# Turning the exponents of two batches, and the first block's normalised rows, by TensorE instead of by DMA

## The chip, the cores and the metric

The kernel runs on one core of one Trainium2 chip. The metric is the time of one execution on the device in microseconds (us), as the median over several runs. A profiled execution, taken by the hardware profiler, stands beside it; all rows shown here come from that execution. The engines are named as in the profile: PE is TensorE's matrix multiplication, PEld its load of the stationary operand, DVE is VectorE, ACT is ScalarE, POOL is GpSimd, and SP is the engine whose queue issues most DMAs.

## The reference

Four batches of 576 tokens pass through four steps. First comes attention with 8 heads of 64 columns, masked by blocks of 64 tokens, in 32 bits:

```python
scores = scale * np.matmul(q, k.transpose(0, 1, 3, 2))
scores = np.where(mask, scores, -1000000000.0)
scores = scores - np.max(scores, axis=-1, keepdims=True)
attn = np.exp(scores)
attn = attn / (np.sum(attn, axis=-1, keepdims=True) + 1e-09)
return np.matmul(attn, v)
```

Then comes a normalisation over the 512 columns, with a feed-forward layer 512 to 2048 to 512 behind it and a residual sum; then a two-dimensional Fourier transform of which the real part is added; then a second normalisation and feed-forward layer. The change touches the attention of the first 256 tokens of batches 0 and 1, and the normalisation in front of the first feed-forward layer for batch 0's first 256 tokens.

## The kernel before

The tokens are cut into blocks: E b holds tokens 0 to 255 of batch b (b is 0 to 3), F b and L the others. Attention of the E blocks runs first, a pair of heads p at a time (four pairs for a batch). A later stream does the attention of the other tokens. The first feed-forward layer takes its blocks in the order E0, E1, E2, E3, F0, and so on.

Matrix products keep nearly 32 bits by splitting each operand into a high and a low half of 16 bits and adding three products (high by high, high by low, low by high). So an operand of a product is first split by an ACT pass (the high half) and a DVE pass (the rest), and what has to be turned is turned as 16-bit halves by a transposing DMA on SP's queue.

For one pair of heads of an E block the steps are these. `e_raw` loads queries and keys in 32 bits by three DMAs and clears half of the key tiles on POOL. `e_s` multiplies them on PE, in 32 bits, into the PSUM tile `st` (two buffers), and `mask` adds the block mask. `e_exp` takes the row maxima (DVE) and the exponents (ACT) into `e`, 128 rows by 768 columns. `e_norm_p` splits `e` into the 16-bit tile `P` by `p_split` (L885 on ACT, L886 on DVE) and turns it by `p_turn`, a transposing DMA of 128 by 1536 elements (L892). `e_pv` multiplies the turned tile `PT` with the values on PE (L861, 18 products of at most 65 columns; column 65 is of ones and gives the row sums), and `e_x` divides and writes the block `X`. `e_load` brings a batch's values in one DMA (L836) into the tile `rv`, of which there is one buffer; `e_v` scales and splits them (L870, L873, L874, a sum over all partitions on POOL, and five small DVE steps).

`ln` makes a block's row means and scales, `ln_hi` the normalised rows `xn` and their high half `xs` (L568), `ln_lo` the low half (L574) and two transposing DMAs into `xnT` (L575). `gemm1` then multiplies `xnT` with the layer's first weights (L607), eight groups of 24 products, two groups for each quarter of the weights.

Beside this runs the decoding of the first layer's weights. `w_load` brings a piece of 1 MB (L198), `w_decode` makes 32-bit numbers of it (ACT L213, DVE L214, ACT L235), and `w_hi` and `w_lo` scale and split each quarter (ACT L327, DVE L335). `gemm1` of a quarter waits for that quarter.

Which work is laid beside which is set by `merge`: each stream has a start time and a rate in planned units, and the item with the earliest planned time is emitted next. E0 starts at 0, the weights at 20, E1 at 25, E2 and E3 at 50. Every engine then carries out its own instructions in the order that the build laid down, and waits at the head of its queue. `prio(f, n)` lets what f emits go n places earlier in that order. The E blocks' tiles come from a pool with a fixed number of buffers for each tag:

```python
a_open(dict(stage=ST, rv=RVE, raw=RAWE, vh=2, vl=2, e=E1B[0], P=E1B[1], PT=E1B[2], xnT0=1, xn0=X0B, xs0=X0B))
```

Here `rv` has one buffer, `raw` two, `e` three, `P` and `PT` two each.

Of the kernel before, what the change touches and what calls it, by code (L numbers as in the profile page):

```python
# [8 lines left out]
F32 = mybir.dt.float32  # L9
F16 = mybir.dt.float16  # L10
# [3 lines left out]
AF = mybir.ActivationFunctionType  # L14
ALU = mybir.AluOpType
# [3 lines left out]
DM = H * D  # L19
FF = 4 * DM  # L20
NPAIR = H // 2
KT = DM // 128
# [5 lines left out]
ST = 2  # L28
RVE = 1
RAWE = 2  # L30
# [11 lines left out]
E1B = (3, 2, 2)  # L42
NB = 1
P_D = 0
EL = 1
RKB = 2
PSC = 2.0 ** 14
WN = (2, 1)
# [5 lines left out]
X0B = 2  # L54
G1E = 1
LNA = 2
ESP = 20
# [38 lines left out]
def fused_kernel(ctx: ExitStack, tc: tile.TileContext, io: dict):  # L96
    nc = tc.nc
# [4 lines left out]
    fpool = ctx.enter_context(tc.tile_pool(name="fpool", bufs=1))  # L102
# [413 lines left out]
    xnT = {}  # L516
# [36 lines left out]
    def ln_hi(ffn, c, t):  # L553
        mv, y = lnst[ffn, c]
        own = (ffn, c) == (1, ("E", 0))
        if own:
            xn = a_tile([128, DM], F32, "xn0", "xn0")
        else:
            xn = fpool.tile([128, DM], F32, tag="xn", bufs=1, name="xn")
        nc.vector.tensor_scalar(  # L560
            out=xn, in0=X[c][:, t, :], scalar1=mv[:, t, 0:1], scalar2=y[:, t:t + 1],
            op0=ALU.subtract, op1=ALU.mult,
        )
        if own:
            xs = a_tile([128, 2, DM], F16, "xs0", "xs0")
        else:
            xs = fpool.tile([128, 2, DM], F16, tag="xs", bufs=1, name="xs")
        nc.scalar.activation(out=xs[:, 0, :], in_=xn, func=AF.Copy)  # L568
        lnst[ffn, c, t] = (xn, xs)

    def ln_lo(ffn, c, t):
        xn, xs = lnst.pop((ffn, c, t))
        eng = nc.gpsimd if (ffn, t) in LNP else nc.vector
        eng.tensor_tensor(out=xs[:, 1, :], in0=xn, in1=xs[:, 0, :], op=ALU.subtract)  # L574
        nc.sync.dma_start_transpose(  # L575
            out=xnT[ffn, c].rearrange("p a k t -> p (a k) t")[:, :, t * 128:(t + 1) * 128],
            in_=xs.rearrange("p a f -> p (a f)"),
        )
# [206 lines left out]
    A = {}  # L785
# [10 lines left out]
    def a_open(bufs):  # L796
        ap_["ctx"] = ExitStack()
        ap_["p"] = ap_["ctx"].enter_context(tc.tile_pool(name="apool", bufs=1))
        ap_["b"] = bufs

    def a_tile(shape, dt, tag, name):
        return ap_["p"].tile(shape, dt, tag=tag, bufs=ap_["b"][tag], name=name)
# [29 lines left out]


    def e_load(b):
        r = a_tile([128, NPAIR, 256], F32, "rv", f"rv{b}")
        nc.sync.dma_start(  # L836
            out=r.rearrange("k p (c d) -> k p c d", c=2),
            in_=io["vt"][b].rearrange("p k c d -> k p c d")[:, :, 0:2, :],
        )
        A["rv", b] = r  # L840
# [24 lines left out]
    def e_v(b):  # L865
        r = A.pop(("rv", b)).rearrange("k p (n d) -> k (p n) d", d=64)
        vh, vl = v_tiles(4 * NPAIR, f"{b}")
        vhf, vlf = vh[:, :, 0:64], vl[:, :, 0:64]
        n2 = sm.tile([128, 1], F32, tag="en", name="en")
        nc.scalar.activation(out=vhf, in_=r, func=AF.Square, accum_out=n2)  # L870
        tot = all_sum(n2, 1, "et")
        s, _ = pow2(tot, 1, "e")
        nc.scalar.activation(out=vhf, in_=r, func=AF.Copy, scale=s)  # L873
        nc.vector.scalar_tensor_tensor(  # L874
            out=vlf, in0=r, scalar=s, in1=vhf, op0=ALU.mult, op1=ALU.subtract
        )
        A["ev", b] = (vh, vl, s)
# [17 lines left out]
    def weights_of(sums, sv, shape, tag):  # L895

        w = sm.tile([128, 2] + shape, F32, tag="rr" + tag, bufs=3, name="rr")
        t, r = w[:, 0], w[:, 1]
        nc.vector.tensor_scalar(
            out=t, in0=sums, scalar1=1e-9 * PSC, scalar2=sv, op0=ALU.add, op1=ALU.mult  # L900
        )
        nc.vector.reciprocal(out=r, in_=t)
        return r
# [17 lines left out]
    def e_exp(b, p):  # L921
        st = A.pop(("st", b, p))
        e = a_tile([128, 2, 384], F32, "e", "e")
        q = sm.tile([128, 2, 2, 2], F32, tag="eq", bufs=3, name="eq")
        mx, nb = q[:, 0], q[:, 1]
        for t, (o, w) in enumerate(EO):
            nc.vector.tensor_reduce(out=mx[:, t], in_=st[:, :, o:o + w], axis=AX.X, op=ALU.max)
        nc.vector.tensor_scalar(out=nb, in0=mx, scalar1=-0.125, scalar2=None, op0=ALU.mult)
        for t, (o, w) in enumerate(EO):
            for h in range(2):  # L930
                nc.scalar.activation(
                    out=e[:, h, o:o + w], in_=st[:, h, o:o + w], func=AF.Exp, scale=0.125,
                    bias=nb[:, t, h:h + 1],
                )
        A["e", b, p] = e

    def e_norm_p(b, p):
        e = A.pop(("e", b, p))
        P = a_tile([128, 2, 768], F16, "P", "P")
        p_split(e.rearrange("p h k -> p (h k)"), P, 768)  # L940
        A["PT", b, p] = p_turn(P, 12)

    @(lambda f: prio(f, EPP))
    def e_pv(b, p):
        vh, vl, s = A["ev", b]
        PT = A.pop(("PT", b, p)).rearrange("k (a h c) q -> k a h c q", a=2, h=2)
        ps = pso.tile([128, 2, 2, 65], F32, tag="o", name="pv")
        for t in range(2):
            for h in range(2):
                mm = []  # L950
                for c in range(t + 1):
                    n = 4 * p + 2 * c + h
                    for a, v, w in ((0, vh, 65), (0, vl, 64), (1, vh, 65)):
                        mm.append((PT[:, a, h, t + c], v[:, n], w))
                pv(ps[:, t, h], mm)
        A["pv", b, p] = (ps, s)

    @(lambda f: prio(f, EXP))
    def e_x(b, p):
        ps, s = A.pop(("pv", b, p))  # L960
        c = ("E", b)
        if p == 0:
            x_alloc(c)
        r = weights_of(ps[:, :, :, 64:65], s, [2, 2, 1], "e")
        nc.vector.tensor_tensor(
            out=X[c][:, :, 128 * p:128 * p + 128].rearrange("p t (h d) -> p t h d", h=2),
            in0=ps[:, :, :, 0:64], in1=r.to_broadcast([128, 2, 2, 64]), op=ALU.mult,
        )

    def e_items(b):  # L970
        def head():
            e_raw(b, 0)
            e_load(b)

        def front(p):
            if p + 1 < NPAIR:
                e_raw(b, p + 1)
            e_s(b, p)
            e_exp(b, p)
            e_norm_p(b, p)  # L980

        def back(p):
            e_pv(b, p)
            e_x(b, p)

        out = [(0.0, head, (), None), (3.0, lambda: front(0), (), None), (1.0, lambda: e_v(b), (), None)]
        for p in range(1, NPAIR):
            out.append((3.0, lambda p=p: (front(p), back(p - EL) if p >= EL else None), (), None))
        for p in range(NPAIR - EL, NPAIR):
            out.append((1.0, lambda p=p: back(p), (), ("X1", ("E", b)) if p == NPAIR - 1 else None))  # L990
        return out
# [455 lines left out]
    if True:  # L1447
# [28 lines left out]
            dft_setup(dctx)  # L1476

        ap_["first"] = True
        a_open(dict(stage=ST, rv=RVE, raw=RAWE, vh=2, vl=2, e=E1B[0], P=E1B[1], PT=E1B[2], xnT0=1, xn0=X0B, xs0=X0B))
        w_signs(ap_["p"], WN[0], NZ[0])  # L1480
        AE = [e_items(b) for b in range(B)]
        A1 = [(0.0, a_switch, (("W", 1, 2, 3), ("X1", ("E", 3))), None)]
# [114 lines left out]
def _consts():  # L1597
    k = np.arange(289)
    n = np.arange(288)
    ang = 2 * np.pi * ((n[:, None] * k[None, :]) % 576) / 576.0  # L1600
    ct, sn = _hl(np.cos(ang)), _hl(np.sin(ang))
    sn[:, :, 0] = 0
    sn[:, :, 288] = 0
    c = {}
    for nm, m in (("ct", ct), ("sn", sn)):
        if nm == "ct":
            m = m.copy()
            m[:, 0, 1::2] = 0
        c[nm] = m[:, :256].reshape(2, 2, 128, 289).transpose(2, 1, 0, 3)
        c[nm + "l"] = np.concatenate([m[0, 256:], m[0, 256:], m[1, 256:]])  # L1610
    row = np.zeros((2, 289), np.float16)
    row[:, 1::2] = CS
    c["ctl"] = np.concatenate([c["ctl"], row])
    f = np.arange(256)
    l = np.arange(257)
    cd = _hl(np.cos(2 * np.pi * ((f[:, None] * l[None, :]) % 512) / 512.0))
    c["cd"] = cd.reshape(2, 2, 128, 257).transpose(2, 1, 0, 3)
    f = np.arange(1, 257)
    l = np.arange(1, 256)
    sd = _hl(np.sin(2 * np.pi * ((f[:, None] * l[None, :]) % 512) / 512.0))  # L1620
    sd[:, 255] = 0
    c["sd"] = sd.reshape(2, 2, 128, 255).transpose(2, 1, 0, 3)
    row = np.zeros((1, 289), np.float16)
    row[0, 0:257] = CS * (1 - 2 * (np.arange(257) % 2))
    c["row"] = row
    return {"c_" + nm: np.ascontiguousarray(v) for nm, v in c.items()}


# [60 lines left out]
```

## Time and profile before

| what | value |
|---|---|
| median of three runs | 1006.12 us |
| lowest and highest | 1006.08 and 1009.24 us |
| the profiled execution's own time | 1002.97 us |
| its span on the core | 1001.1 us |
| busy: PE, DVE, ACT, POOL | 920.1, 714.8, 544.2, 86.0 us |
| DMA packets | 173022, of which 146957 under 512 B |

The span is what the profile shows from the first to the last instruction; the rest of the profiled execution's own time lies around it. PE is busy for 92% of the span, but not evenly: in the first 75 us it is busy for 46 us. A clock throttle grants PE either of two levels, 1.2 or 2.4 GHz, so the same instruction has two durations.

### The profile page before, as it was taken

The numbers are of one execution on the slowest core, as the hardware profiler recorded it, in microseconds if no ns is written. First come the engines' busy times: TensorE is split into PE (matmuls) and PEld (weight loads), VectorE is DVE, ScalarE is ACT, GpSimd is POOL, SyncE is SP. The second block draws the span as 40 slices with busy tenths as digits, with TensorE's granted clock in tenths as the row PEclk, the third lists the DMA queues.
The fourth block names the chain that finished last, engine by engine and source line by source line (L and its number), as shares of the span: only waits on it lengthen the run. The fifth ranks groups of instructions, "written<-read, shape, count | busy, mean of one in ns | idle before, by whom it ended". The sixth has DMA issues, their size and how long they took to land.

```text
span 1001.1 us, 19763 instructions
## 1 busy us (share of the span) xinstructions
PE 920.1 (92%) x7730; PEld 692.0 (69%) x7730; DVE 714.8 (71%) x1773; ACT 544.2 (54%) x969; POOL 86.0 (9%) x217
## 2 busy tenths in 40 slices
PE   5486979998998989999899889999999999999998
PEld 4375754575575665676576665858588888888887
DVE  4789687686977876675677887769576775765754
ACT  5678575777687677636656554325153352442431
POOL 2101001001002001040011120100000000000000
PEclk9678899999999999999999999999999999999999
DMA  7997743667668657359408557111110101101100
GB/s 216 244 272 201 213 96 113 132 130 129 156 124 171 124 130 146 70 144 321 138 15 243 184 192 237 41 23 64 43 23 22 33 22 33 22 23 43 22 23 22
DMA packets 173022, 115.11 MB, mean 115 GB/s; under 512 B 146957, under 2 KB 155158, under 8 KB 170880
## 3 DMA queue, kind: packets, MB, share of 16 engines
q1 hardware_dynamic: 170608, 109.59, 42.4%
q0 software_dynamic: 2320, 4.25, 1.7%
q8 instruction: 61, 1.00, 0.4%
q14 instruction: 33, 0.27, 0.1%
HBM read 64.13 MB, written 11.01 MB: 75 GB/s over the span
## 4 chain that ended last, share of the span: by engine, by line
PE 44%; DVE 6%; DMA 5%; ACT 2%; issue 1%; POOL 0%; SPq 0%; ACTq 0%; DVEq 0%; POOLq 0%
PE g L678 15%; PE s L728 13%; PE g L607 7%; PE g L659 4%; PE g L632 3%; DMA wr<-in_w 3%; DVE wq L335 1%; ACT junk L235 1%; DVE ws L214 1%; ACT sign L213 1%; PE ya L1352 1%; DMA xnT2('F', 0)_8438<-xs 1%; DVE hT L617 1%; DMA d<-ws 1%; PE pq L1386 0%
## 5 line engine op out<-in xcount | busy, mean ns | idle before, releaser
L607 PEld LDWEIGHTS <-wq 128*128 128x128 f16 x2112 | 208.1, 100 | 47.3 <-issue 6.1
L632 PE MATMUL g<-wq,hT 128*128 128x512 f16 x768 | 185.8, 380 | 2.6 <-ACT hT L616 2.2
L678 PEld LDWEIGHTS <-wq 128*128 128x128 f16 x1344 | 131.5, 98 | 15.4
L632 PEld LDWEIGHTS <-hT 128*128 128x128 f16 x768 | 74.1, 98 | 86.7 <-issue 4.8
L861 PE MATMUL pv<-vh,PT 128*128 128x65 f16 (+1 forms) x800 | 105.1, 202 | 24.4 <-DMA PT<-P 21.7
L695 ACT ACTIVATE hr<-g,tk 128x256 f32<-128x256 f32 x112 | 47.0, 470 | 144.4 <-PE g L678 144.4
L728 PEld LDWEIGHTS <-hs 128*128 128x128 f16 x1176 | 115.1, 98 | 13.3
L861 PEld LDWEIGHTS <-PT 128*128 128x128 f16 x1200 | 83.7, 100 | 50.0 <-DMA PT<-P 23.7
L703 DVE TENSOR_TENSOR hr<-hr 128x128 f32<-128x128 f32 x224 | 65.4, 292 | 48.3 <-ACT hr L695 40.3
L1073 PE MATMUL st<-k,qz 128*128 128x512 f16 (+2 forms) x288 | 80.6, 333 | 15.4 <-ACT e L1095 15.4
L886 DVE SCALAR_TENSOR_TENSOR P<-e,P 128x768 f16<-128x768 f32 (+2 forms) x64 | 61.9, 970 | 39.5 <-ACT P L885 39.3
L1095 ACT ACTIVATE e<-st,aq,acf 128x384 f32<-128x384 f32 (+2 forms) x80 | 56.8, 740 | 58.6 <-DVE aq L1090 51.8
L728 PE MATMUL s<-tT,hs 128*128 128x256 f16 x672 | 75.6, 273 | 0.0
L617 DVE SCALAR_TENSOR_TENSOR hT<-g,hT 128x512 f16<-128x512 f32 x88 | 59.8, 683 | 20.1 <-ACT hT L616 20.0
L616 ACT ACTIVATE hT<-g 128x512 f16<-128x512 f32 x88 | 51.2, 586 | 37.0 <-PE g L607 36.9
L861 PE MATMUL pv<-vl,PT 128*128 128x64 f16 (+1 forms) x400 | 65.4, 202 | 0.1
L659 PE MATMUL g<-wq,hT 128*128 128x512 f16 x288 | 64.4, 379 | 0.5 <-DVE wq L335 0.5
L710 DVE TENSOR_TENSOR hs<-hr,hs 128x896 f16<-128x896 f32 x56 | 60.8, 1085 | 0.5
L213 ACT ACTIVATE sign<-wr 128x512 f16<-128x512 bf16 (+1 forms) x48 | 46.4, 970 | 26.5 <-DMA wr<-in_w 21.2
L728 PE MATMUL s<-tB,hs 128*128 128x256 f16 x504 | 57.3, 273 | 0.0
L885 ACT ACTIVATE P<-e 128x768 f16<-128x768 f32 (+2 forms) x64 | 54.5, 859 | 4.1 <-DMA PT<-P 2.5
L214 DVE SCALAR_TENSOR_TENSOR ws<-wr,sign 128x512 int32<-128x512 int32 (+1 forms) x48 | 41.3, 865 | 20.1 <-ACT sign L213 17.7
(414 smaller groups left out, 1578.2 us busy)
## 6 DMA issues: line engine op xcount, KB each, us to landing
wr<-in_w SPq DMA_DIRECT2D x16, 1023.5 KB, 6.0
wr<-in_w SPq DMA_DIRECT2D x32, 511.8 KB, 5.2
rawv<-in_vt SPq DMA_DIRECT2D x16, 320.0 KB, 3.6
rawqk<-in_kt SPq DMA_DIRECT2D x16, 288.0 KB, 2.8
d<-ws SPq DMA_DIRECT2D x4, 1024.0 KB, 5.0
ws<-d SPq DMA_DIRECT2D x4, 1024.0 KB, 5.2
wt<-d SPq DMA_DIRECT2D x4, 1024.0 KB, 4.9
rawqk<-in_qt SPq DMA_DIRECT2D x32, 80.0 KB, 3.3
```

The lines of the kernel that those rows point to most:

```text
L607: nc.tensor.matmul(out=ps[:, i, :], lhsT=w1(ffn, k, wh, m), rhs=xt[:, xh, k, :], start=(n == 0), stop=(n == 3 * KT - 1),)
L617: nc.vector.scalar_tensor_tensor(out=h[:, :, 1, :], in0=ps, scalar=0.0, in1=h[:, :, 0, :], op0=ALU.max, op1=ALU.subtract,)
L632: nc.tensor.matmul(out=ps, lhsT=h[f // 4][:, f % 4, hh, t * 128:(t + 1) * 128], rhs=w2(ffn, f, wh), start=(f == 0 and hh == 0 and wh == 0) ...
L659: nc.tensor.matmul(out=g2["b"][t], lhsT=h[f // 4][:, f % 4, hh, t * 128:(t + 1) * 128], rhs=w2(ffn, f, wh), start=(f == 0 and hh == 0 and ...
L678: nc.tensor.matmul(out=ps[:, q, :], lhsT=w1(2, k, wh, i + 8 * q), rhs=xt[:, xh, k, :], start=(n == 0), stop=(n == 3 * KT - 1),)
L703: done = nc.vector.tensor_tensor(out=r[:, o], in0=r[:, a], in1=r[:, b], op=op)
L710: nc.vector.tensor_tensor(out=h[:, 1], in0=r[:, 1:8], in1=h[:, 0], op=ALU.subtract)
L728: nc.tensor.matmul(out=ps, lhsT=h[:, hh, hb], rhs=T[nm][:, wh, i], start=(i == 0 and hh == 0 and wh == 0), stop=(i == 7 and hh == 1),)
L861: nc.tensor.matmul(out=out[..., 0:w], lhsT=l, rhs=v[..., 0:w], start=(n == 0), stop=(n == len(mm) - 1))
L886: nc.vector.scalar_tensor_tensor(out=P[:, 1, 0:n], in0=e, scalar=PSC, in1=P[:, 0, 0:n], op0=ALU.mult, op1=ALU.subtract)
L1073: nc.tensor.matmul(out=st[:, h, 0:n] if j < 4 else sf[:, o:o + n], lhsT=qz[:, a, q:q + 128], rhs=k[:, c, o:o + n], start=(i == 0), stop=(j ...
L1095: nc.scalar.activation(out=e[:, h], in_=st[:, h], func=AF.Exp, scale=cf, bias=nb[:, h:h + 1],)
```

## The change

For batches 0 and 1 (`ET`), the exponents `e` stay in 32 bits. Six products on PE with a 128 by 128 unit matrix in 32 bits turn them into the PSUM tile `st` that held the scores, one ACT copy brings them to `PT` (now 32 bits), and `e_pv` does six products in 32 bits where it did 18 in 16 bits. The values are used as they come: `e_v` falls away, and `e_load` brings them by four DMAs with a gap of two columns for the ones, where it brought them by one. The `rv` buffer now holds the values until the last `e_pv` of the batch. For block E0, four products with the unit matrix turn each half of `xn` into PSUM, from which ACT writes the high half and DVE the low half straight into `xnT`. The unit matrix is one more DMA, on POOL's queue, ahead of POOL's other work. Batches 2 and 3 and the other blocks stay as they were.

```diff
+ET = (0, 1)
...
         if own:
-            xs = a_tile([128, 2, DM], F16, "xs0", "xs0")
-        else:
-            xs = fpool.tile([128, 2, DM], F16, tag="xs", bufs=1, name="xs")
+            return ln_turn(ffn, c, t, xn)
+        xs = fpool.tile([128, 2, DM], F16, tag="xs", bufs=1, name="xs")
...
+    def ln_turn(ffn, c, t, xn):
+
+        ps = g_tile([128, 4, 128], "xt")
+        for k in range(KT):
+            nc.tensor.matmul(
+                out=ps[:, k], lhsT=xn[:, 128 * k:128 * k + 128], rhs=A["unit"],
+                start=True, stop=True,
+            )
+        to = xnT[ffn, c][:, :, :, t * 128:(t + 1) * 128]
+        nc.scalar.activation(out=to[:, 0], in_=ps, func=AF.Copy)
+        nc.vector.tensor_tensor(out=to[:, 1], in0=ps, in1=to[:, 0], op=ALU.subtract)
...
     def e_load(b):
+        if b in ET:
+            r = a_tile([128, NPAIR * 4, 66], F32, "rv", f"rv{b}")
+            nc.gpsimd.memset(r[:, :, 64:65], 1.0)
+            for p in range(NPAIR):
+                nc.sync.dma_start(
+                    out=r[:, 4 * p:4 * p + 4, 0:64],
+                    in_=io["vt"][b, p][:, 0:2, :].rearrange("k c (h d) -> k (c h) d", h=2),
+                )
+            A["ev", b] = r
+            return
...
+    def e_turn(b, p):
+
+        e, st = A.pop(("e", b, p))
+        for h in range(2):
+            for o in range(0, 384, 128):
+                nc.tensor.matmul(
+                    out=st[:, h, o:o + 128], lhsT=e[:, h, o:o + 128], rhs=A["unit"],
+                    start=True, stop=True,
+                )
+        et = a_tile([128, 2, 384], F32, "PT", "PT")
+        nc.scalar.activation(out=et, in_=st[:, :, 0:384], func=AF.Copy)
+        A["PT", b, p] = et
...
     def e_norm_p(b, p):
+        if b in ET:
+            return prio(e_turn, ESP)(b, p)
...
     def e_pv(b, p):
+        if b in ET:
+            v, e = A["ev", b], A.pop(("PT", b, p))
+            ps = pso.tile([128, 2, 2, 65], F32, tag="o", name="pv")
+            for t in range(2):
+                for h in range(2):
+                    for c in range(t + 1):
+                        nc.tensor.matmul(
+                            out=ps[:, t, h], lhsT=e[:, h, 128 * (t + c):128 * (t + c) + 128],
+                            rhs=v[:, 4 * p + 2 * c + h, 0:65], start=(c == 0), stop=(c == t),
+                        )
+            A["pv", b, p] = (ps, None)
+            return
...
-        out = [(0.0, head, (), None), (3.0, lambda: front(0), (), None), (1.0, lambda: e_v(b), (), None)]
+        out = [(0.0, head, (), None), (3.0, lambda: front(0), (), None)]
+        if b not in ET:
+            out.append((1.0, lambda: e_v(b), (), None))
...
-        a_open(dict(stage=ST, rv=RVE, raw=RAWE, vh=2, vl=2, e=E1B[0], P=E1B[1], PT=E1B[2], xnT0=1, xn0=X0B, xs0=X0B))
+        a_open(dict(stage=ST, rv=RVE, raw=RAWE, vh=2, vl=2, e=E1B[0], P=E1B[1], PT=E1B[2], xnT0=1, xn0=X0B, unit=1))
+        A["unit"] = a_tile([128, 128], F32, "unit", "unit")
+        nc.gpsimd.dma_start(out=A["unit"], in_=io["c_unit"])
```

## Rows read from the trace of the kernel before

**Rows 1.** The profile's page, part 1: busy time, share of the span, instructions.

```profile
PE 920.1 (92%) x7730; PEld 692.0 (69%) x7730; DVE 714.8 (71%) x1773; ACT 544.2 (54%) x969; POOL 86.0 (9%) x217
```

**Rows 2.** Windows of 25 us: busy time by engine, granted PE clock, DMA share, GB/s.

```profile
0.00:25.00 25.00, 14.65 (x84) 11.45 (x84) 12.47 (x37) 14.30 (x26) 5.97 (x19) 0.90 0.75 215
25.00:50.00 25.00, 10.29 (x85) 8.54 (x86) 19.38 (x61) 16.70 (x28) 4.08 (x12) 0.64 0.91 245
50.00:75.00 25.00, 21.38 (x201) 17.73 (x199) 20.06 (x44) 19.54 (x29) 1.18 (x4) 0.78 0.99 272
75.00:100.00 25.00, 17.06 (x118) 13.51 (x117) 23.13 (x66) 22.19 (x36) 3.95 (x12) 0.84 0.78 200
100.00:125.00 25.00, 23.70 (x239) 19.96 (x240) 16.14 (x44) 13.64 (x20) 1.81 (x6) 0.89 0.74 216
```

**Rows 3.** Groups by line, first 75 us: busy us, mean ns, idle before with releasers.

```profile
L913 PEld LDWEIGHTS st<-raw 128*128 128x128 f32 x64 | 15.3, 287 | 12.5 <-POOL raw L848 5.6 <-issue 5.5 <-POOL vh L855 0.2
...
L861 PE MATMUL pv<-vh,PT 128*128 128x65 f16 x96 | 7.6, 218 | 15.6 <-DMA PT<-P 15.6
L886 DVE SCALAR_TENSOR_TENSOR P<-e,P 128x768 f16<-128x768 f32 x8 | 7.6, 949 | 0.0
L885 ACT ACTIVATE P<-e 128x768 f16<-128x768 f32 x8 | 6.9, 862 | 0.1
...
L870 ACT ACTIVATE vh<-rv 128x1024 f16<-128x1024 f32 x3 | 3.2, 1059 | 5.0 <-DMA rv<-in_vt 5.0
...
L874 DVE SCALAR_TENSOR_TENSOR vl<-rv,pw,vh 128x1024 f16<-128x1024 f32 x2 | 2.6, 1285 | 0.7 <-ACT vh L873 0.7
L616 ACT ACTIVATE hT<-g 128x512 f16<-128x512 f32 x4 | 2.5, 618 | 4.0 <-PE g L607 4.0
```

**Rows 4.** Timeline of PE: start us, us for all, instruction, count, idle before.

```profile
9.36 2.06 PE L913 MATMUL st<-raw 128*128 128x256 f32 x4
...
12.03 0.93 PEld L913 LDWEIGHTS st<-raw 128*128 128x128 f32 x4 [0.67 <-POOL raw L848]
...
16.27 1.35 PE L913 MATMUL st<-raw 128*128 128x256 f32 x4
...
22.68 1.00 PEld L861 LDWEIGHTS <-PT 128*128 128x128 f16 x18 [4.30 <-DMA PT<-P]
...
37.54 0.53 PEld L913 LDWEIGHTS st<-raw 128*128 128x128 f32 x4
...
71.73 0.69 PEld L861 LDWEIGHTS <-PT 128*128 128x128 f16 x18
```

**Rows 5.** Waits of SP's queue, first 150 us: us in total, times, longest.

```profile
SPq L892 <- DVE P L886: 15.6, 7, 4.4
```

**Rows 6.** Timeline of several engines, at the waits that end last.

```profile
31.05 0.22 DVE L899 TENSOR_SCALAR rr<-pv,pw 128x4 f32<-128x4 f32 x1 [2.58 <-PE pv L861]
...
33.11 1.36 ACT L213 ACTIVATE sign<-wr 128x1024 f16<-128x1024 bf16 x1 [3.45 <-DVE ws L214]
...
56.19 2.08 PE L607 MATMUL g<-xnT,wq 128*128 128x256 f16 x9 [1.77 <-DMA xnT<-xs]
...
63.80 1.34 ACT L931 ACTIVATE e<-st,eq 128x128 f32<-128x128 f32 x4
...
84.92 6.41 PEld L607 LDWEIGHTS <-wq 128*128 128x128 f16 x44 [0.27 <-DVE wq L335]
...
99.94 5.30 PE L607 MATMUL g<-xnT1('E', 1)_796,wq 128*128 128x256 f16 x24 [2.17 <-DMA xnT1('E', 1)_796<-xs]
```

**Rows 7.** The page's DMA issues: count, KB each, median us to landing.

```profile
rv<-in_vt SPq DMA_DIRECT2D x4, 512.0 KB, 4.9
...
PT<-P SPq DMA_TRANSPOSE x64, 4.2
...
xnT<-xs SPq DMA_TRANSPOSE x2, 5.8
```

**Rows 8.** Timeline of POOL: a DMA that POOL issues.

```profile
445.48 0.57 POOL L1244 DMA_DIRECT2D c_ct<-in_c_ct  x1
```

More of the change, by code (lines that the diff above doesn't have):

```diff
@@ L564, in ln_hi @@
         if own:
-            xs = a_tile([128, 2, DM], F16, "xs0", "xs0")
-        else:
-            xs = fpool.tile([128, 2, DM], F16, tag="xs", bufs=1, name="xs")
+            return ln_turn(ffn, c, t, xn)
+        xs = fpool.tile([128, 2, DM], F16, tag="xs", bufs=1, name="xs")
         nc.scalar.activation(out=xs[:, 0, :], in_=xn, func=AF.Copy)
         lnst[ffn, c, t] = (xn, xs)
+    def ln_turn(ffn, c, t, xn):
[8 more added lines that the diff above has]
+        nc.vector.tensor_tensor(out=to[:, 1], in0=ps, in1=to[:, 0], op=ALU.subtract)
     def ln_lo(ffn, c, t):
+        if (ffn, c) == (1, ("E", 0)):
+            return
         xn, xs = lnst.pop((ffn, c, t))
@@ L934, in e_exp @@
                 )
-        A["e", b, p] = e
+        A["e", b, p] = (e, st) if b in ET else e
+    def e_turn(b, p):
[9 more added lines that the diff above has]
+        A["PT", b, p] = et
     def e_norm_p(b, p):
+        if b in ET:
+            return prio(e_turn, ESP)(b, p)
         e = A.pop(("e", b, p))
@@ L944, in e_pv @@
     def e_pv(b, p):
+        if b in ET:
[9 more added lines that the diff above has]
+            A["pv", b, p] = (ps, None)
+            return
         vh, vl, s = A["ev", b]
@@ L963, in e_x @@
             x_alloc(c)
-        r = weights_of(ps[:, :, :, 64:65], s, [2, 2, 1], "e")
+        if s is None:
+            w = sm.tile([128, 2, 2, 2, 1], F32, tag="rre", bufs=3, name="rr")
+            r = w[:, 1]
+            nc.vector.tensor_scalar(
+                out=w[:, 0], in0=ps[:, :, :, 64:65], scalar1=1e-9, scalar2=None, op0=ALU.add
+            )
+            nc.vector.reciprocal(out=r, in_=w[:, 0])
+        else:
+            r = weights_of(ps[:, :, :, 64:65], s, [2, 2, 1], "e")
         nc.vector.tensor_tensor(
@@ L1625, in _consts @@
     c["row"] = row
+    c["unit"] = np.eye(128, dtype=np.float32)
     return {"c_" + nm: np.ascontiguousarray(v) for nm, v in c.items()}
```

## The prediction

> **What bounds the kernel now.** I began with the page's busy times. PE is busy for 92% of the span [rows 1], so the kernel is one long row of products, and it can end earlier only if PE's dense stretch begins earlier or loses work. The windows show where that stretch begins. In the first 75 us PE works for 14.65, 10.29 and 21.38 us, 46.3 in all, and has 28.7 us free; from 100 us on it is busy for 23.70 of 25 [rows 2]. Everything that the change touches lies in these first 75 us. So the question is not what PE's added work costs as such, but what holds the first `gemm1` back.
>
> I then read the waits that end last on the way there [rows 6]. The second half of E0's products loads its weights at 84.92 us, and the releaser is `wq`, the decoded weight, on DVE. E1's products start at 99.94 us, held last by the turned rows of E1. The weights are decoded by ACT and DVE in turn, with the attention's instructions between theirs. In the windows from 25 to 100 us these two are the fullest engines: DVE 19.38, 20.06, 23.13 of 25 us, ACT 16.70, 19.54, 22.19 [rows 2]. The time there goes by in three ways: their own work, waits of one for the other, and waits for transposing DMAs. Three waits are of the third kind. DVE waits 2.58 us for `pv` of E0's third pair, and the weight step behind it lets ACT wait 3.45 us at 33.11 us; `pv` itself waits for `PT`, 15.6 us over the 75 us [rows 3, 6]. PE waits for `xnT` before E0's first products at 56.19 us [rows 6], and ACT, with its other work done, waits 4.0 us for the first output of these (L616) [rows 3]. SP's queue stands for 15.6 us with a transpose at its head, waiting for DVE's half of `P` [rows 5], and key loads and weight pieces are queued behind it. The DMA engines are 0.91 and 0.99 busy from 25 to 75 us [rows 2].
>
> **The price of a 32-bit product.** The trace has 32-bit products: those of `e_s` (L913). Each program product appears as two load and product pairs (128 loads for 64 products over the kernel, of which 64 loads here [rows 3]). The loads set the pace at 128 columns. Four of them take 0.93 us at the low level and 0.53 at the high one [rows 4], so one product of 128 columns or fewer costs 2 x 0.23 = 0.46 us or 2 x 0.13 = 0.27 us. `e_turn` is six products, 12 loads: 2.8 or 1.6 us for a pair. The new `e_pv` has no row for 65 columns in 32 bits. From below it could cost what its halved count gives at 16 bits, 12 of 18 loads of 1.00 us, 0.7 us; from above the same 2.8 us as the turn. I take the upper end at each level, 2.8 or 1.6, because the load of 128 columns is the same instruction as in L913. It replaces 18 products at 1.00 us (low) or 0.69 (high) [rows 4].
>
> The Trainium skill ("FP8 and Floating Point Precision", TensorE Precision Notes) says that true 32-bit products make four passes through the array. By that, an estimate, 65 columns take 4 x 65 cycles, 0.11 us at 2.4 GHz, six of them 0.65 us a pair instead of 1.6, and PE would get 7.6 us less new work. The row speaks for the loads as the pace at so few columns. The sum below does not rest on it, for in the forecast this work lies in PE's free time.
>
> PE's new load is then 8 pairs x 24 loads and 16 for E0's rows, 208 loads: 27.6 us at the high level less 8 x 0.69 = 5.5, so 22 us more; at the low level 48.4 less 8.0, so 40 us more. The free 28.7 us cover the first and not the second; that is the second rival.
>
> **The change part by part, on the path to the dense stretch.**
>
> *Turning `e`.* Before, from `e` to `pv`: ACT 0.86, DVE 0.95 [rows 3], issue to landing 4.2 [rows 7], 6.0 us in all. After: turn 1.6 to 2.8, ACT copy. No row copies 768 columns from PSUM; 512 take 0.62 us (L616), 768 from SBUF 0.86 (L885) [rows 3]. I take 0.86, the same width. That is 2.5 to 3.7 us, so 2.3 to 3.5 us less. On the path this shortens ACT's 3.45 us at 33.11: a gain of 2.3 to 3.45. I take 2.5, since PE is mostly at the low level from 25 to 50 us (granted clock 0.64 [rows 2]). For the last pair of E1 the gain is larger (its exponents start at 63.80 and take 1.34, its `pv` starts at 71.73 [rows 4, 6]: 6.6 us against 2.5), which brings E1's normalisation, the other gate, forward by 4.1 us more than the weights; so the weights stay the gate that counts.
>
> *Turning E0's rows.* ACT's and DVE's halves cost the same as before, only from PSUM. The transposes' 5.8 us [rows 7] give way to four products for each half, 1.06 to 1.9 us, so 3.9 to 4.7 less; what this can give the weights is ACT's idle 4.0 us. Taken: 4.0, bounds 3.9 and 4.0.
>
> *Work taken from ACT and DVE.* ACT loses 8 x 0.86 and two passes of 1024 columns in each batch (1.06 for the one, the other put at the same): 6.9 + 4.2. It gains eight copies, 6.9. DVE loses 8 x 0.95 + 2 x 1.28 = 10.2 us [rows 3]. POOL loses two sums over partitions. ACT was busy for 50.5 of the first 75 us [rows 2], two thirds, so I count two thirds of its 4.2, 2.8 us, and nothing of DVE's, which waits for ACT in the same chain. Bounds: nothing, and 4.2.
>
> *DMA.* Eight transposes of 393 KB and two of 262 KB, 3.7 MB, leave SP's queue and the DMA engines, of the 18.3 MB that the first three windows move. With them goes the standing of SP behind DVE in these two batches. I count nothing for it: the wait ahead of the weight step at 33.11 is for DVE, not for the weight's DMA [rows 6]. If loads are what comes next, this is a gain that the sum lacks, and the reason why the range goes lower.
>
> *What is added at the start.* The unit matrix is one issue on POOL's queue, 0.57 us [rows 8], ahead of the clearing of the key tiles on which the first scores wait. SP has three more issues for the values before the second pair's keys and the first weight piece, put at the same 0.57, 1.7 us; the later transposes gone from the queue give some of it back. Taken: 0.6 + 0.9; bounds 0.6 and 2.3.
>
> *A new wait on PE.* The turn stands in PE's order behind the scores of its pair and waits for ACT's exponents (1.34 us [rows 6]), and `e_pv` waits for the copy (0.86); E0's `gemm1` products are queued behind both. Two pairs of E1 fall beside them: at most 4.4 us. I take 1.3, nearer to nothing, because `gemm1` has to wait for its last quarter of weights anyway; if the weights come early this cover is gone and the 4.4 count.
>
> Sum: -2.5 - 4.0 - 2.8 + 1.5 + 1.3 = -6.5 us. With every bound at its better end it is -3.45 - 4.0 - 4.2 + 0.6 = -11.1, at its worse end -2.3 - 3.9 + 2.3 + 4.4 = +0.5. Behind 100 us nothing is changed and PE is full, so I carry the shift to the end unchanged. Against the profiled execution's own 1002.97 us this gives 996.5. The median of the runs is 3.15 us above that execution, so in its terms 1006.12 - 6.5, 1000 us, with 995 to 1006.6 as the forecast's own range.
>
> **The rivals.** *The gain is used up before the dense stretch* (0.18). From 75 to 100 us DVE is busy for 23.13 of 25 [rows 2], with work of E2 and the second weights that the change leaves; if that work's loads do not come earlier, E1's products still start near 99.9 us. For it speaks that E1's own rows are still turned by DMA, at whose end E1's products start [rows 6]. Against it speaks that X of E1 comes earlier by both gains. Time: a shift of -2 to +1, so 1004 to 1007.
>
> *PE becomes the bound of the first 75 us, at the low level* (0.12). Then 40 us of new work meet 28.7 free, and 11 us stick out: 1017. It decides from 0.176 us for a load on ((28.7 + 8.0) / 208), a little under half way from the high to the low price. For it: the granted clock of 0.64 from 25 to 50 us [rows 2]. Against it: four products of 256 columns took 2.06 us at 9.36 and 1.35 at 16.27 [rows 4], and PE did 32-bit scores and masks alone until then, so such work does raise the clock; and more of it leaves fewer pauses. The Trainium skill ("TensorE: Matmul & The Clock Gate", Part 4: PE-mode transpose) states that transposes on PE do not engage the full clock; it speaks of the transpose mode, which these plain products with a unit matrix do not use, and by it this rival's 1017 would be the time.
>
> *The single buffer of the values* (0.10). It is now held until the batch's last `pv`. The values of batch 2 can be asked for only after `pv` of E1's last pair (71.73 before [rows 4]), and then need 4.9 us [rows 7] and 1.7 for the added issues in the batches where there are four. SP and POOL are in order: keys and weight pieces queued behind that load wait with it, and ACT's pass over these values has weight steps behind it. From about 6.5 us of such waiting on, the gain is gone; both batches together at 6.6 us each give +6.7: 1013. Against it: SP already stood there for DVE's half of `P` [rows 5].
>
> **From these to the numbers.** A measurement here can tell about 0.3%, 3 us, from no change. The forecast has 0.60, of which 0.05 lies within 3 us. Faster: 0.55 and 0.02 of the first rival, 0.57. Same: 0.05, 0.14 of the first rival and 0.03 of the last, 0.22. Slower: 0.21. The range goes down to 991, for a DMA gain on top of a good sum, and up to 1011, short of the full price of the last two rivals.
>
> **What would show it.** In the changed profile `wq` should release E0's last products some 6 us before 84.92, and E1's products should start near 93 instead of 99.94. ACT's 4.0 us ahead of L616 and its 3.45 at the third weight piece should be gone or under 1. New rows should show the turn at 1.6 to 2.8 us a pair and PE's granted clock from 25 to 50 us above 0.64. I am wrong if PE is above 24 of 25 us in the second or third window, if a wait for the values' DMA or for `rv` stands on SP, POOL or ACT for several us, or if the start of E1's products moves and the end does not.

## The result and the profile after

The changed kernel took 991.99 us (median of four runs, 991.83 to 999.0), beside 1006.1 us for the kernel before (1001.37 to 1009.24): a ratio of 0.9891, 95% interval 0.9864 to 0.9918. Six later runs of the same program gave 997.76 us (996.23 to 998.85) beside 1005.90, a ratio of 0.9912, interval 0.9892 to 0.9931, and so 8.8 us with 6.9 to 10.8. (The ratios come from runs taken side by side; they are not quotients of the two medians, which here differ by 8.1 us.) The profiled execution after is one of the first four: 991.83 us, span 990.1.

The page's busy times after, against [rows 1]: DVE and ACT lose some work, PE gains 5.8 us.

```profile
PE 925.9 (94%) x7794; PEld 701.4 (71%) x7794; DVE 706.0 (71%) x1753; ACT 541.5 (55%) x963; POOL 85.6 (9%) x216
```

The windows of 25 us after, with the columns of [rows 2]. PE works for 59.4 us in the first 75, where it had 46.3. The granted clock, 0.64 and 0.78 in the second and third window before, is 1.00 in this execution, the upper of its two levels (2.4 GHz). The DMA share falls from 0.91 and 0.99 to 0.71 and 0.59.

```profile
0.00:25.00 25.00, 16.29 (x99) 14.58 (x100) 7.50 (x24) 10.21 (x19) 6.44 (x21) 1.00 0.70 220
25.00:50.00 25.00, 19.06 (x160) 17.32 (x160) 21.13 (x65) 20.89 (x33) 3.37 (x11) 1.00 0.71 225
50.00:75.00 25.00, 24.03 (x213) 21.54 (x212) 20.85 (x58) 21.61 (x33) 1.99 (x6) 1.00 0.59 196
75.00:100.00 25.00, 18.52 (x171) 15.22 (x172) 20.47 (x46) 21.74 (x35) 2.85 (x7) 0.93 0.93 247
100.00:125.00 25.00, 22.74 (x243) 19.00 (x240) 22.78 (x72) 20.10 (x35) 2.89 (x9) 1.00 0.61 151
```

The groups of the first 75 us after. The turn (L966) and the values' products (L990) are new; the 15.6 us for which PE waited for `PT` [rows 3] are now 0.3 us, and 8.0 us of waiting for exponents stand ahead of the turn. ACT's idle ahead of `hT`, 4.0 us at L616 in [rows 3], is 0.7.

```profile
L966 PE MATMUL st<-unit,e 128*128 128x128 f32 x96 | 13.9, 300 | 8.0 <-ACT e L955 8.0
...
L990 PE MATMUL pv<-rv,PT 128*128 128x65 f32 x96 | 12.1, 275 | 0.3 <-ACT PT L971 0.2
...
L971 ACT ACTIVATE PT<-st 128x768 f32<-128x768 f32 x8 | 6.5, 813 | 1.0 <-PE st L966 1.0
...
L630 ACT ACTIVATE hT<-g 128x512 f16<-128x512 f32 x6 | 3.6, 600 | 0.7 <-PE g L621 0.6
```

PE's timeline after. A turn of one pair takes 2.93 us at the start, where its products run at the slow pace, and 1.60 later; the values' products take 1.55. The last quarter of E0's weights (44 of its 192 products are left; the prediction calls it the second half) comes at 74.95 us instead of 84.92, and E1's products start at 88.17 instead of 99.94 [rows 6], again held last by the DMA that turns E1's rows.

```profile
11.79 2.93 PE L966 MATMUL st<-unit,e 128*128 128x128 f32 x12 [4.05 <-ACT e L955]
...
19.71 1.60 PE L966 MATMUL st<-unit,e 128*128 128x128 f32 x12
...
31.07 1.55 PE L990 MATMUL pv<-rv,PT 128*128 128x65 f32 x12 [0.24 <-ACT PT L971]
...
74.95 0.55 PEld L621 LDWEIGHTS <-wq 128*128 128x128 f16 x6 [0.32 <-DVE wq L336]
...
88.17 2.10 PE L621 MATMUL g<-xnT1('E', 1)_683,wq 128*128 128x256 f16 x9 [5.13 <-DMA xnT1('E', 1)_683<-xs]
```

ACT's timeline after. The 3.45 us of [rows 6] stood ahead of the sign pass, the first of the decoding, of the fourth weight piece (the signs start at 14.10, 22.89, 28.32 and 33.11 us before). That wait is gone, yet the fourth sign starts only 0.36 us sooner, at 32.75: ACT now does the passes of the first quarter (L328, from 30.91 us) ahead of it, where they stood behind it (L327, from 34.33 us). New is the table load at 9.08 us, right in front of the first exponents.

```profile
9.08 1.28 ACT L955 ACT_TABLE_LOAD   x1 [9.08 <-DVE eq L952]
10.38 1.36 ACT L955 ACTIVATE e<-st,eq 128x128 f32<-128x128 f32 x4
...
28.03 1.37 ACT L214 ACTIVATE sign<-wr 128x1024 f16<-128x1024 bf16 x1
...
30.91 1.93 ACT L328 ACTIVATE wq<-ws,gs 128x512 f16<-128x512 f32 x3
32.75 1.35 ACT L214 ACTIVATE sign<-wr 128x1024 f16<-128x1024 bf16 x1
```

In the kernel before the table load lay under the wait of ACT's first pass over the values for their DMA, and cost nothing:

```profile
0.73 1.28 ACT L870 ACT_TABLE_LOAD   x1 [0.73 <-PEq L1659]
7.07 1.06 ACT L870 ACTIVATE vh<-rv 128x1024 f16<-128x1024 f32 x1 [5.05 <-DMA rv<-in_vt]
```

Where the stages start, in one profiled execution of each of these kernels (start of the block's first product of the feed-forward layer, and the span, us; the later stages are the same code in all):

| kernel | E0 | E1 | E2 | F1 | L | second layer | span |
|---|---|---|---|---|---|---|---|
| before | 56.2 | 99.9 | 197.5 | 413.9 | 461.9 | 627.6 | 1001.1 |
| changed | 45.9 | 88.2 | 182.7 | 399.5 | 450.8 | 616.7 | 990.1 |
| changed, again | 49.0 | 91.4 | 187.1 | 403.8 | 455.2 | 623.4 | 996.8 |
| rows only | 57.5 | 99.7 | 192.0 | 408.9 | 459.7 | 624.7 | 998.5 |
| exponents only | 53.7 | 91.3 | 187.6 | 404.5 | 455.1 | 624.4 | 998.2 |
| TensorE's work only | 58.8 | 95.8 | 192.6 | 408.2 | 459.4 | 624.2 | 1000.4 |
| turn twice | 58.0 | 100.3 | 196.4 | 415.2 | 465.3 | 631.0 | 1004.3 |

### The profile page after: what moved, and what is told of

Read it like the earlier page. It is cut to its first block, busy times and chain, and to the rows that moved or that the text cites. A ratio compares the mean times of both kernels' runs of the same rounds, so it can differ in the third digit from the quotient of the medians.

```text
span 990.1 us, 19844 instructions
## 1 busy us (share of the span) xinstructions
PE 925.9 (94%) x7794; PEld 701.4 (71%) x7794; DVE 706.0 (71%) x1753; ACT 541.5 (55%) x963; POOL 85.6 (9%) x216
## 4 chain that ended last, share of the span: by engine, by line
PE 47%; DVE 5%; DMA 4%; ACT 3%; issue 1%; POOL 0%; SPq 0%; ACTq 0%; POOLq 0%; DVEq 0%
PE g L692 15%; PE s L742 13%; PE g L621 9%; PE g L673 4%; PE g L646 4%; DMA wr<-in_w 3%; PE ya L1413 1%; ACT junk L236 1%; DVE ws L215 1%; DVE wq L336 1%; ACT sign L214 1%; DMA xnT2('F', 0)_8352<-xs 1%; DMA d<-ws 1%; PE pq L1447 0%; PE pv L885 0%
## 5 line engine op out<-in xcount | busy, mean ns | idle before, releaser
L885 PE MATMUL pv<-vh,PT 128*128 128x65 f16 (+1 forms) x704 | 97.2, 200 | 8.7 <-DMA PT<-P 4.6
L885 PEld LDWEIGHTS <-PT 128*128 128x128 f16 x1056 | 76.0, 98 | 34.2 <-issue 11.7
L910 DVE SCALAR_TENSOR_TENSOR P<-e,P 128x768 f16<-128x768 f32 (+2 forms) x56 | 54.4, 974 | 33.7 <-ACT P L909 33.4
L630 ACT ACTIVATE hT<-g 128x512 f16<-128x512 f32 x88 | 51.3, 587 | 30.6 <-PE g L621 30.4
L885 PE MATMUL pv<-vl,PT 128*128 128x64 f16 (+1 forms) x352 | 58.2, 199 | 0.0
L723 ACT ACTIVATE hs<-hr 128x896 f16<-128x896 f32 x56 | 53.2, 949 | 1.6 <-DVE hr L717 1.6
```

The lines of the kernel that those rows point to most:

```text
L885: nc.tensor.matmul(out=out[..., 0:w], lhsT=l, rhs=v[..., 0:w], start=(n == 0), stop=(n == len(mm) - 1))
```

## The experiments

Each kernel ran beside the kernel before, and ratios are against that. The changed kernel's own ratio, for comparison, is 0.9912. One thing weighs on all of them: the order of each engine's queue is worked out anew for every program, so an edit also moves instructions that it does not name. The ratios differ from the quotients of the medians by up to 0.0016, so a difference of 1 or 2 us between two kernels is not to be read from them.

**Rows only, and exponents only.** The change has two halves; each alone.

```diff
-ET = (0, 1)      # rows only
+ET = ()
...
-            return ln_turn(ffn, c, t, xn)      # exponents only
+            xs = a_tile([128, 2, DM], F16, "xs0", "xs0")
...
```

> Only E0's normalised rows are turned by TensorE; the exponents of all four batches go by DMA as before. If the sum's terms hold, this is the -4.0 us of the rows (about 1002), less the start of the unit matrix. If the gain is one of the attention alone (waits behind its transposes, or its work on ACT and DVE), it lies within 1 us of before, 1006, since the weights' last quarter still ends late; then E0's first products start earlier than 56.19 but its last ones do not move from 84.92.

> Only the exponents of batches 0 and 1 are turned by TensorE; E0's rows go by DMA. If the two parts add, this is after plus 4 us, 996. If the attention is all of it, 992 to 993. If the rows are what lets the rest through, 1002 or more.

Rows only: 1000.31 us, ratio 0.9945 (0.9916 to 0.9973), 5.5 us less. Exponents only: 996.29 us, 0.9904 (0.9873 to 0.9936), 9.7 us less. The exponents' half alone does as much as the whole; the two do not add at the end of the span. The rows' half has the mean granted clock of the kernel before, 0.972 in both (medians of the runs), though its profiled execution has 0.70 and 0.90 in the second and third window where [rows 2] has 0.64 and 0.78. At E2's start the table has -5.5 and -9.9 for the halves, and -14.8 and -10.4 for the two executions of the whole.

**The values still split.** ACT's two passes, DVE's pass and POOL's sums over the values come back, into tiles that nobody reads.

```diff
-        if b not in ET:
-            out.append((1.0, lambda: e_v(b), (), None))
+        out.append((1.0, lambda: (e_v_extra if b in ET else e_v)(b), (), None))
```

> After, with the values of batches 0 and 1 scaled and split as before into tiles that nothing reads: per batch two ACT passes, one sum over partitions and six DVE steps are put back, 4.6 us of ACT and 4.2 us of DVE in all. If work on ACT and DVE is what the first 75 us are made of, 995 to 997 (about a third of the gain goes). If waits behind the transposes are what counted, 992 to 994.

1000.13 us, 0.9932 (0.9907 to 0.9956): 2.0 us more than the changed kernel's ratio. The intervals overlap, so it bears out a cost of about the forecast's size and does not show it.

**The transposes kept.** In the place of each removed transpose SP issues one of a tile of ones, whose result nobody reads; then the same with 128 x 128 in place of 128 x 1536 elements.

```diff
         A["PT", b, p] = et
+        jt = a_tile([128, 12, 128], F16, "jt", "jt")
+        nc.sync.dma_start_transpose(out=jt, in_=A["still"].rearrange("p a k -> p (a k)"))
...
```

> After, with the eight transposing DMAs of 128 by 1536 put back on SP's queue from a tile of ones into a tile that nothing reads: the queue and the DMA engines carry what they carried, and nobody waits for the turned tile. If the gain came from room on the DMA engines and in SP's queue (counted at nothing in the sum), 996 to 1000. If it came from the way of the exponents alone, 992 to 994.

> The changed kernel, with eight transposing DMAs on SP's queue whose result nobody reads, at the places of the removed ones, each of 128 x 128 elements in place of 128 x 1536. Theory that the places on SP's queue and their issue times cost the 8 us that the eight large ones cost: 998 to 1000 us here too. Theory that the 16 DMA engines' time costs them (a large one keeps them busy for some us, a small one for a twelfth): 992 to 994 us.

Large: 1000.07 us, 0.9938 (0.9915 to 0.9961). Small: 997.73 us, 0.9927 (0.9904 to 0.9951). The "8 us" of the second expectation was the distance to the first four runs of the changed kernel. Against its ratio from six more runs the large transposes cost 2.6 us and the small ones 1.5, with intervals that overlap its own. That room on SP's queue and on the DMA engines is the main gain, to which the first of these runs seemed to lead, is not borne out; a part of a few us stays possible.

**The changed kernel again.** No edit.

> The changed kernel itself, so that the experiments have a base of more than four runs. If its first runs were typical: 991 to 993 us. The executions of one kernel so far go along with the mean clock that was granted to TensorE (two value buffers: 990.4 us at 0.989, 1001.8 us at 0.979), and three of the four first runs had 0.989 or more; if those were luck, the median is 994 to 997 us, and the costs of the experiments measured against it shrink by 3 to 5 us.

997.76 us: the first four were on the lucky side. The two profiled executions of this one program show where they part. Until 35 us they have the same instructions in the same order, 0.28 us apart; then PE waits 2.88 us for exponents in both. First the execution of 991.83 us, then that of 998.54: PE's timeline.

```profile
37.64 1.60 PE L966 MATMUL st<-unit,e 128*128 128x128 f32 x12 [2.88 <-ACT e L955]
41.40 2.06 PE L575 MATMUL xt<-unit,xn 128*128 128x128 f32 x16 [2.15 <-DVE xn L561]
...
45.93 1.15 PE L621 MATMUL g<-xnT,wq 128*128 128x256 f16 x9
```

```profile
37.92 2.93 PE L966 MATMUL st<-unit,e 128*128 128x128 f32 x12 [2.88 <-ACT e L955]
41.68 3.78 PE L575 MATMUL xt<-unit,xn 128*128 128x128 f32 x16 [0.83 <-DVE xn L561]
...
48.96 1.15 PE L621 MATMUL g<-xnT,wq 128*128 128x256 f16 x9
```

The windows of PE alone around that wait, of the slower one (after the colon: us, busy us, products, granted clock, DMA share, GB/s). In the quicker one the clock is 1.00 in every one of them.

```profile
20.00:35.00 15.00, 13.68 (x110) 1.00 0.80 257
35.00:38.00 3.00, 0.12 (x3) 0.88 0.82 202
38.00:42.00 4.00, 3.17 (x13) 0.50 0.97 297
42.00:46.00 4.00, 4.00 (x20) 0.50 0.86 301
46.00:50.00 4.00, 4.00 (x31) 0.81 0.13 18
```

After the same wait the one keeps the upper level and the other drops to 0.50, the lower one (1.2 GHz), for the turn, the rows' products and the values' products. E0's first product then starts 3.0 us later; 0.3 of that was there before the wait, so the drop costs 2.7 us. The two executions are 4.4 us apart at E2 and 6.7 at the end, but that is not this one drop: 2.3 us of it arise between block L and the second layer, where the clock is 0.86 from 575 to 600 us and 0.98 in the quicker one.

**Two value buffers.**

```diff
-RVE = 1
+RVE = 2
```

> The values of a batch get two 32-bit buffers in place of one, so the second batch's values need not wait for the first batch's last product. The forecast's theory: ScalarE waited 0.4 us for values in the changed kernel, so the time stays at 991 to 993 us. The rival of the single buffer: values that come late hold up the second batch's products and the queue behind them, and two buffers give 2 to 4 us back: 988 to 990 us.

999.89 us (990.38 to 1002.95), 0.9945 (0.9912 to 0.9978): no gain. Yet the second batch's values are asked for 9 us sooner, as SP's timeline shows, first in the changed kernel and then here:

```profile
32.65 2.03 SPq L853 DMA_DIRECT2D rv<-in_vt  x4
```

```profile
23.53 3.37 SPq L853 DMA_DIRECT2D rv<-in_vt  x4
```

So the single buffer does hold these loads up, and no cost of it shows in the time; from 41 us on PE's order is another here too. Time and mean granted clock mostly go together from run to run: 990.38 us at 0.989 and 993.14 at 0.990, but 1001.76 at 0.979 and 1002.95 at 0.981; a run of 1002.83 at 0.986 does not fit. In its trace the wait of 2.88 us also ends in a turn of 2.93 us.

**TensorE's work only.** The kernel before, and on top the turn's products, written over the scores and read by nobody. Transposes, normalisation and split stay.

```diff
+        e, st = A.pop(("e", b, p))
+        if b < 2:
+            prio(e_fill, ESP)(b, p, e, st)      # the six products of the turn
...
```

> The kernel before, with the turn's products on TensorE for both batches (96 products, 13 to 23 us by the clock) written into the scores' bank and read by nobody; the transposing DMAs, normalisation and split stay. If a TensorE that works more keeps its clock in the first 75 us (0.90, 0.64 and 0.78 before) and the kernel gains from that alone: 995 to 1002 us. If that work stands in the queue ahead of what sets the path, as the doubled turn did: 1006 to 1015 us.

1001.69 us (1000.74 to 1002.5), 0.9954 (0.9937 to 0.9970): 4.6 us less than the kernel before, with 48 more products (96 in the trace, which shows a 32-bit product twice) and nothing removed. Its windows show a clock of 0.86 where [rows 2] has 0.64, 0.78 and 0.84:

```profile
0.00:25.00 25.00, 15.30 (x102) 13.11 (x102) 12.69 (x36) 14.79 (x25) 7.39 (x22) 1.00 0.90 226
25.00:50.00 25.00, 16.64 (x154) 14.77 (x155) 21.59 (x64) 19.39 (x33) 3.00 (x10) 0.86 0.91 248
50.00:75.00 25.00, 18.05 (x186) 15.52 (x185) 20.41 (x49) 20.65 (x31) 1.55 (x5) 0.86 1.08 311
75.00:100.00 25.00, 19.96 (x150) 16.40 (x148) 21.88 (x59) 19.93 (x31) 3.43 (x9) 0.86 0.80 231
```

The clock is not all that differs. PE and ACT have their instructions in another order, and in the first 75 us PE waits 8.6 us for `PT` in place of 15.6. E0's first product starts later than before (58.8 after 56.2), and the gain shows from E1 on (95.8 after 99.9). So it is shown that this program is faster in spite of its added products; that the higher clock is the reason is likely, but no run parts it from the new order.

**The turn twice.** The changed kernel with each of the turn's products issued twice.

```diff
-        for h in range(2):
+        for h in (0, 1, 0, 1):
```

> Every product of the turn is issued twice, so TensorE does some 8 x 1.6 = 13 us more in the first 75 us; nothing else changes. If TensorE's new work is hidden behind the waits of the first 50 us (it is busy 16.3 and 19.1 of 25 us there in the changed kernel), only the pairs turned in the dense third stretch (24.0 of 25 us) cost anything: 993 to 997 us. If TensorE bounds the first stage, as the rival with its price of 8 to 13 us says, the time rises by most of it: 1000 to 1005 us.

1008.1 us, 1.0038 (1.0019 to 1.0056), 12.7 us more than the changed kernel's ratio. The group of the turn is 27.9 us in place of 13.9 and 16.0 in the two executions of the changed kernel, so 12 to 14 us were added and the time rises by as much, although the clock stays high (1.00, 0.93, 1.00 in the first three windows). PE's order is another here too. ACT's copies now wait for the turn, 6.2 us in all:

```profile
L966 PE MATMUL st<-unit,e 128*128 128x128 f32 x192 | 27.9, 300 | 5.3 <-ACT e L955 5.3
...
L971 ACT ACTIVATE PT<-st 128x768 f32<-128x768 f32 x8 | 6.5, 812 | 6.2 <-PE st L966 6.2
```

**Three attempts to go further.** The table load brought forward; the same together with E1's rows by TensorE; the exponents of all four batches by TensorE.

```diff
+        wake = cpool.tile([128, 1], F32, name="wake")      # table early
+        nc.scalar.activation(out=wake, in_=gmax, func=AF.Exp)
...
-        own = (ffn, c) == (1, ("E", 0))      # rows of E1
+        own = ffn == 1 and c in (("E", 0), ("E", 1))
...
-ET = (0, 1)      # all four
+ET = (0, 1, 2, 3)
```

> The changed kernel with one exponential of a single column at the very start, which brings ScalarE's table load (1.28 us at 9.08 us) ahead of the first exponents. Theory that the first exponents are on the path: 1 us less than the changed kernel. Rival, that the order of TensorE's queue, which the planner makes anew with each edit, decides more than that: a difference of 2 to 8 us of either sign.

> The changed kernel with two additions: E1's rows of the first layer too are turned by TensorE and split from PSUM, and one exponential of a single column at the very start brings the table load (1.28 us at 9.08 us in the changed kernel) ahead of the first exponents. Theory that the wait for E1's transposing DMAs (5.1 us at 88 us) and the table load stand on the path: 985 to 988 us. Rival, that the weight stream through SP's queue bounds the stage up to E2 and the wait only moves to the next weight piece: 990 to 993 us.

> The exponents of all four batches of the first block are turned by TensorE. The pairs of batches 2 and 3 run after 75 us, where TensorE is busy 23 of 25 us: 8 x 1.6 us of turning and the 32-bit values products come on top there, so 1000 to 1010 us. Rival, that the removed transposes and the split's work of batches 2 and 3 pay as those of the first two did: 985 to 990 us.

Table early: 1004.76 us, 0.9978 (0.9951 to 1.0005), 6.6 us more than the changed kernel's ratio. The first exponents do start sooner, at 9.20 us, but PE's new order has the first pair's values products in front of the second pair's scores, and the second exponents start at 20.14 us, after 18.30 in the changed kernel. ACT's timeline:

```profile
9.20 1.36 ACT L955 ACTIVATE e<-st,eq 128x128 f32<-128x128 f32 x4 [6.97 <-DVE eq L952]
...
20.14 1.36 ACT L955 ACTIVATE e<-st,eq 128x128 f32<-128x128 f32 x4 [4.52 <-DVE eq L952]
```

With E1's rows as well: 1007.46 us, 1.0021 (1.0004 to 1.0038). The wait for E1's DMA is gone, but in PE's queue E1's rows now stand ahead of E0's last 120 products of `gemm1`. PE's timeline: after 64.7 us the next of them starts at 87.55, behind scores that wait for keys and behind those rows:

```profile
77.22 0.76 PE L937 MATMUL st<-raw 128*128 128x128 f32 x2 [2.85 <-DMA raw<-in_kt]
...
82.13 3.51 PE L575 MATMUL xt<-unit,xn 128*128 128x128 f32 x16 [2.07 <-DVE xn L561]
...
87.55 10.66 PE L621 MATMUL g<-xnT,wq 128*128 128x256 f16 x96 [0.39 <-DVE xnT1('E', 1)_686 L581]
```

All four: 999.33 us, 0.9933 (0.9914 to 0.9952), no better than two. E2's first product is at 194.1 us, 7.0 later than in the second execution of the changed kernel. No version beat the changed kernel.

## Why the prediction was right, and where its sum was not

The direction was right. The forecast's -6.5 us stands against 8.8 us less (6.9 to 10.8), so the sum is a little small, and that it came near is partly luck: the two halves measured alone make 5.5 and 9.7 us, 15.2 together, where the forecast has 4.0 and 2.5, and the whole gives less than their sum.

**The rows of E0, -4.0:** right in size for that half alone, which gave 5.5 us (2.7 to 8.4), and in part in its way. ACT's 4.0 us of idle time went, and there the last of E0's products starts at 84.4 us after 91.3. But E0's first product starts no sooner (57.5 after 56.2), and E1's do not move (99.7 after 99.9), held by their own rows' DMA as the first rival had it; the gain shows only at E2 (192.0 after 197.5), and no run shows by which step. On top of the exponents' half, the ends show nothing more from it.

**The exponents' half** is the term that was mis-sized: -2.5 for the turn, -2.8 for the work taken, +1.5 and +1.3 make -2.5, and it measured 9.7 us (6.4 to 12.8). Two things were wrong in it. First, TensorE's clock had no term. The prediction expected it above 0.64 and used it only to price the rival. The kernel with products read by nobody is 4.6 us faster at a higher clock, which is the largest part found, though its order is another. The two executions of the changed kernel, one program with one order, show the price of a drop there: 2.7 us for one that begins behind one wait. The clock is not the whole: the rows alone gained at the mean clock of the kernel before, and the doubled turn is the slowest kernel at a mean clock of 0.987. How much of the 9.7 us is the clock stays open.

Second, the turn was counted once, on the one wait of 3.45 us, and "in the forecast this work lies in PE's free time" gave the products no price of their own. The doubled turn speaks against such cover in the changed kernel: with 12 to 14 us more work it took 12.7 us longer. If the turns are on the way, so is the gain of the shorter way from `e` to `pv`, for more than one pair. This is argued, not shown, since the doubled turn also has another order, and it does not hold for every pair: behind the turn at 37.64 us, PE waits another 2.15 us for `xn`. The wait of 3.45 us that the term was taken from was also read as the third weight piece's; it is the fourth's, whose sign starts only 0.36 us sooner after the change.

**Durations** held: the turn 1.60 and 2.93 us (forecast 1.6 and 2.8), the values' products 1.55 (1.6; 2.82 at the low level with two value buffers), the copy 0.81 (0.86). The Trainium skill ("FP8 and Floating Point Precision", TensorE Precision Notes) counts four passes, by which, an estimate, 65 columns take 0.11 us; the trace has 1.55 us for six such products, 0.26 each, so the loads set the pace and the measurement decides.

**Work taken from ACT and DVE, -2.8:** giving it back cost 2.0 us with overlapping intervals; not contradicted. **DMA, counted at nothing:** 1.5 to 2.6 us, not separable from nothing; what parts three of the first four runs, at 992, from the later ones goes with the clock (0.989 to 0.991 against 0.982 to 0.986), not with the DMA gain that was the reason given for the lower end of the range.

**The start, +1.5:** the first values' product came 0.8 us later (18.31 after 17.51), but not for POOL's unit matrix, which moved the first scores by 0.2 (4.25 after 4.01). The table load of 1.28 us, which the sum did not see, stands ahead of the first exponents, and they start 1.45 us later (10.38 after 8.93); that it is the larger share is not shown, since PE's order differs there. **The wait on PE, +1.3:** it exists, 8.0 us in four waits for exponents; its price was not measured by itself. The longest of them next to E0's products, 2.88 us, held nothing up in the quicker execution, since PE then waits 2.15 us more for DVE's `xn`.

**The shift carried to the end** held only in part: 14.4 us at F1, 11.1 at block L, 11.0 at the end. The loss is between F1 and L: 51.3 us after, 48.0 before. There ACT waits for a DMA that turns rows of L. It was issued at 446.85 us and took 7 us before; after, it was issued at 431.85 and took 12. In both, SP issues eight of the second layer's weight loads right behind it. ACT's timeline, before and after:

```profile
453.82 0.63 ACT L568 ACTIVATE xs<-xn 128x512 f16<-128x512 f32 x1 [3.61 <-DMA xnT1L<-xs]
```

```profile
443.93 0.63 ACT L568 ACTIVATE xs<-xn 128x512 f16<-128x512 f32 x1 [8.35 <-DMA xnT1L<-xs]
```

Yet every other kernel of the table needs 50.1 to 51.4 us there as well, "TensorE's work only" among them, which removed nothing. The kernel with all four batches, which has the change too, needs 48.0 us (411.1 to 459.1) with a wait of 3.38 us at that place, so the change does not have to cost this. What decides it stays open.

**The rivals.** The gain was not used up before the dense stretch: E1's products moved by 8.5 to 11.8 us. The low clock did not come (0.80 to 1.00 in place of 0.64), so not the 11 us of the second rival; but its core, that PE has no cover left, is what the doubled turn points to. One argument against it was misread. The four products of 2.06 us at 9.36 and 1.35 at 16.27 [rows 4] do not show the clock rising, for the granted clock of the kernel before is 1.00 in both stretches. Its windows of PE alone:

```profile
8.00:14.00 6.00, 5.33 (x20) 1.00 0.63 227
14.00:20.00 6.00, 4.38 (x35) 1.00 0.84 228
```

On PE transposes and the clock, the rule weighed there (the Trainium skill, "TensorE: Matmul & The Clock Gate", Part 4) does not reach these plain products: the clock was 1.00 from 20 to 35 us, with two turns and the values' products of three pairs. Two signs of being wrong came about, and the time fell all the same. PE was above 24 of 25 us in the third window (24.03, and 24.95 in the second execution), as E0's products had moved into it. And waits for `rv` stood on SP and POOL, until the products that still used the buffer were done; the kernel with two value buffers, which has no first and no third of these, shows no cost of them. The waits in the first 150 us (us in total, times, longest):

```profile
SPq L853 <- PE pv L990: 5.3, 1, 5.3
SPq L860 <- PE pv L990: 4.9, 1, 4.9
POOL rv L851 <- PE pv L990: 5.2, 1, 5.2
```

## What to carry to other kernels

Ask what TensorE's waits do to its clock, and give that a term of its own: here one drop behind one wait cost 2.7 us in one of two executions of the same program, and a kernel with products that nobody read was 4.6 us faster. Whether an added step is under cover can be tried by doubling it, with an eye on what the new order moves, and a saving that repeats in every turn of a loop is not priced by one wait. Where queues are ordered anew for each program, an edit of 1 us can move the end by 6, so take the base as often as the experiments, and look for the first instruction at which two executions part.

## What the runs showed of the hardware

- One program, one wait of 2.88 us on TensorE, two outcomes: the granted clock stayed at 1.00 in one execution and fell to 0.50 for the products behind the wait in another. The drop was worth 2.7 us on the spot; at the end, with later drops, the two were 6.7 us apart.
- The granted clock as the profile gives it does not always tell TensorE's pace: the turn at 11.79 us took 2.93 us, that at 19.71 took 1.60, and the granted clock is 1.00 for both (11.7 to 14.8 us and 19.7 to 21.4). Whether the pace has another cause or the column is not right at the start of an execution is not shown.
- A 32-bit product of 65 columns takes as long as one of 128: 1.55 and 1.60 us for six products, which show as twelve loads and products in the trace.
- ScalarE's table load of 1.28 us is issued with its first activation but ran ahead of that activation's wait for a DMA at 0.73 us before, and behind a wait for DVE at 9.08 us after.
